# A new order of issue for the first 700 operations of an S4 and GEGLU block

## The chip, the cores and the metric

The kernel runs on one core of one Trainium2 chip. The metric is the time of one execution in device microseconds; the time of a kernel is the median of its runs.

## The reference

The input is a sequence of L = 2048 tokens with D = 448 channels. A conditioning vector gives six rows `sa, ca, ga, sb, cb, gb` (a SiLU and one matrix product). The block has two halves:

```
mod = (silu(c) @ w_mod)                          # 6 rows of 448
h = layernorm(x) * (1 + ca) + sa
# S4: a convolution of length 2048 for each channel
P = exp(dt * A * l)                              # 448 x 256 complex states x 2048 steps
K = einsum("dn,dnl,dn->dl", C, P, dt * B).real
y = irfft(rfft(pad(h)) * rfft(pad(K)))[:L] + h * Dskip
x = x + ga * y
h = layernorm(x) * (1 + cb) + sb
x = x + gb * ((gelu(h @ w_gate) * (h @ w_up)) @ w_down)
```

Everything is float32 from outside. The costly parts are the generation of K (complex exponentials for 448 channels and 256 states), the Fourier transforms as matrix products, and the GEGLU with its 1792 hidden features.

## The kernel before

**What is computed when.** The channels are taken eight at a time, in 56 steps `s` (`NSUB`); seven steps make a group `sc`, and two groups share one `prep(t)`, t = 0 to 3. The parts that the first 700 operations come from:

- `prep(t)` turns the complex parameters of 112 channels into the logarithms and phases that the exponentials need. It is a ladder of short steps that hop between VectorE (DVE) and ScalarE (ACT): `p.A1`, `p.A2`, `p.B1`, `p.C2`, `p.D1`, `p.B3`, `p.G1`, `p.E1`, `p.E3` on DVE; `p.S1`, `p.S2` (a logarithm), `p.S3` (an exponential), `p.S4` (an arctangent), `p.A3`, `p.C1`, `p.B2`, `p.E2` on ACT. Its two results are split in three bfloat16 pieces each (`p.c0` to `p.f0`, `p.c1` to `p.f1`; the casts `c` and `e` may run on either engine) and stored to HBM by `p.put0` and `p.put1` beside a constant `pad`. The text calls these steps `A1`, `S1` and so on.
- `load_lt(sc)` (`lt0`, `lt1`) reads them back, rearranged, as matmul operands. `lt0` waits for `p.put0` and for `pad`.
- For each step, TensorE (PE) multiplies them with constants into exponents (`x.mm`, `y.mm`) and angles (`ang`, `anc`); ACT takes exponentials (`x.exp`, `y.exp`) and sines (`sin`, `cos` and, for the first 20 steps, `sin2`, `cos2`); DVE multiplies (`tx`, `tyc`); PE contracts over the states (`kgen`). `kev`, `kd`, `ka` and `kout` turn a pair of steps into spectra of the first kind.
- `mod_row(i)` loads a part of `w_mod` (`m.ld`), multiplies (`m.mm`, or `m.mq0`, `m.cp0` and a sum `m.sm0`) and evacuates (`m.ev`). The products `gs` of two such rows scale the layer norm.
- The tokens: `x.ld`, statistics `bn` on DVE, a square root `rstd` on ACT, `rcp`, `norm` and a scaled constant `as`, the matmuls `ua`, the evacuations `ua.ev`, stores `ua.st`; then the second stage of the transform: `ub.u`, `ub.fc`, `ub`, `ub.ev` or `ub.eg`, `ub.st`.

Behind them follow the spectral products group by group (`f.*`, `t.*`), and then the GEGLU, which fills the rest of the span.

**What sets the order.** There are 2006 operations, and each is issued at a place written out in the table `PLACE`: the n-th number of a name is the place of its n-th call. `Plan.run` sorts by it and issues each operation with all its instructions, so each engine, and the queue of DMA issues on SyncE (SP), gets its own in this order and waits at the head for what is missing.

```
at = PLACE[n][i]
self.at, e = int(at.rstrip("adps")), at[-1]
self.on = {"a": "ACT", "d": "DVE", "p": "POOL", "s": "SP"}.get(e) or next(iter(eng))
```

So a letter behind a number chooses the engine of an operation that may run on two. Buffers are taken and freed in the same order. ACT holds one set of function tables at a time: exponentials, sines and arctangents, the logarithm and the square root are in four sets here, and where the next function is not in the set, a load of a table (`ACT_TABLE_LOAD`) stands ahead of it. Copies, squares and absolute values need none.

Of the kernel before, what the change touches and what calls it, by code (L numbers as in the profile page):

```python
# [40 lines left out]
    "anc": "127 138 148 162 173 210 218 246 266 319 327 332 359 351 433 450 484 460 499 483",  # L41
    "ang": "110 113 140 158 168 164 207 221 247 312 323 331 347 350 423 444 459 448 498 476 508 584 615 595 665 680 663 703 "
        "747 763 768 791 795 815 782 883 889 928 904 914 938 946 1012 1028 1019 1040 1045 1054 1116 1133 1142 1148 1163 "
        "1169 1175 1196",
    "as": "65d 58d 80d 105d 115d 120d 156a 146d 254d 252d 282d 296d 321a 317a 341a 353a",
    "bn": "20 45 24 40 15 17 48 16 215 216 238 245 157 220 194 190",
    "c.ai": "133",
    "c.ak": "231",
    "c.au": "47",
    "c.c": "8",  # L50
    "c.ea": "57",
    "c.ih": "516",
    "c.ld": "4",
    "c.rd": "51",
    "c.t1": "363",
# [21 lines left out]
    "cos": "522 592 638 616 672 699 700 712 762 776 789 814 808 819 796 894 910 942 907 922 945 952 1016 1037 1022 1048 1060 "  # L77
        "1068 1127 1137 1153 1160 1172 1183 1207 1229",
    "cos2": "128 141 152 163 178 211 219 253 272 320 328 343 360 354 440 451 490 467 505 488",
# [3 lines left out]
    "d0": "172",  # L83
# [21 lines left out]
    "dsk": "174",  # L105
# [10 lines left out]
    "ev.ub": "397",  # L116
# [9 lines left out]
    "gs": "66 86",  # L126
# [17 lines left out]
    "ka": "240 279 316 355 381 406 495 525 606 603 710 718 737 832 812 880 917 930 974 1001 1064 1080 1135 1166 1194 1206 "  # L144
        "1242 1246",
    "kd": "200 232 291 346 379 398 469 519 575 579 677 706 736 831 806 879 898 926 970 984 1032 1076 1129 1152 1193 1200 "
        "1240 1245",
    "kev": "199d 230d 290a 345a 378d 393a 462a 518d 548a 577a 654a 705a 735d 818d 805d 853d 897d 924d 969d 983d 1030d 1075d "
        "1113d 1140a 1162a 1191a 1239d 1236a",
    "kgen": "145 181 206 228 243 273 297 322 344 372 376 390 412 419 466 491 517 547 563 576 634 635 679 702 721 722 755 772 "  # L150
        "783 799 822 838 859 896 900 923 937 957 955 982 1025 1026 1049 1058 1086 1105 1128 1139 1158 1161 1181 1190 1199 "
        "1218 1223 1235",
    "kout": "241a 280a 318d 371a 394d 461a 496a 527a 620a 636d 716a 728d 749a 848a 813d 887d 925a 933a 979a 1003a 1069d 1102a "
        "1141a 1167a 1195a 1222a 1244a 1247a",
    "lt0": "64 144 325 368 560 801 861 985",
    "lt1": "92 195 326 369 723 802 968 986",
    "m.cp": "581a 600d 786a",
    "m.cp0": "50d",
    "m.ev": "44 60 63 589 619 804",
    "m.ld": "29 31 30 420 578 760",  # L160
    "m.mm": "43 59",
    "m.mq": "555 599 773",
    "m.mq0": "46",
    "m.sm": "588 618 803",
    "m.sm0": "62",
    "mag": "511a 591a 617a 598d 670d 689a 668a 708a 752d 764a 770a 792a 797d 816a 784a 892a 890d 929a 905a 915a 943a 947a "
        "1013a 1029a 1020d 1041a 1052a 1055a 1117d 1134a 1143a 1149a 1164a 1170a 1185a 1209a",
    "norm": "67 70 99 109 97 121 72 104 237 249 281 287 171 278 227 285",
    "p.A1": "1 88 311 509",
    "p.A2": "7 89 349 531",  # L170
    "p.A3": "25 169 456 481",
    "p.B1": "13 103 365 554",
    "p.B2": "22 155 438 607",
    "p.B3": "23 177 439 613",
    "p.C1": "6 98 416 478",
    "p.C2": "14 106 435 553",
    "p.D1": "32 134 426 571",
    "p.E1": "39 167 437 673",
    "p.E2": "41 185 489 674",
    "p.E3": "42 187 506 686",  # L180
    "p.G1": "38 125 436 623",
    "p.S1": "11 102 358 532",
    "p.S2": "18 116 373 569",
    "p.S3": "21 132 413 570",
    "p.S4": "37 166 434 626",
    "p.al": "2 33 91 474",
    "p.c0": "26a 204d 470a 627a",
    "p.c1": "49a 191d 530d 696d",
    "p.d0": "27 250 493 647",
    "p.d1": "52 258 611 738",  # L190
    "p.e0": "28a 289d 494a 701d",
    "p.e1": "53d 259a 612d 833d",
    "p.f0": "34 298 502 717",
# [1640 lines left out]
```

## Time and profile before

| | |
|---|---|
| median of 3 runs | 777.25 us (776.79 to 779.4) |
| the profiled execution | 776.06 us, of it a span of 774.3 us from the first to the last instruction |
| granted clock of TensorE, mean | 0.995 |
| busy: PE, DVE, ACT | 724.2, 591.3, 459.7 us |
| DMA | 139.87 MB, 181 GB/s over the span |

A row of a group has line, engine, operation, tiles and shapes, the count, then busy us and the mean ns of one, and behind the bar the idle time ahead of them and what ended it. A row of the view in order of time has start and length in us, and in brackets an idle time of the engine ahead of it. A row of the waits has the engine and line that waited, what it waited for, us in total, times and the longest. A row of DMA issues has its size and the us from issue to landing. `q` behind an engine's name is its sequencer; PEld are PE's loads of stationary operands.

### The profile page before, as it was taken

What the parts mean: (1) busy time and instruction counts of PE and PEld (TensorE: products, weight loads), DVE (VectorE), ACT (ScalarE), POOL (GpSimd) and SP (SyncE); (2) the same over time, 40 slices, a digit from 0 to 9 for tenths busy, and PEclk for the clock granted to TensorE, in tenths of its full rate; (3) what the DMA queues carried; (4) which work ended last, traced back from release to release, by engine and by line L of the source; (5) the groups of instructions that cost most, each with busy time, mean ns of one, the idle gap of its engine ahead of it and who ended that gap; (6) DMA issues with size and microseconds to landing.
All of it is one profiled execution on the core that took longest, in us unless ns stands there. A gap on an engine that the chain in (4) does not pass through costs nothing.

```text
span 774.3 us, 19010 instructions
## 1 busy us (share of the span) xinstructions
PE 724.2 (94%) x8166; PEld 442.5 (57%) x8166; DVE 591.3 (76%) x891; ACT 459.7 (59%) x613; POOL 8.5 (1%) x23
## 2 busy tenths in 40 slices
PE   2877889998899999989999999999999999999997
PEld 1333554443677777677874445444694446944487
DVE  6999999999999999979958932578774577144743
ACT  5899999999999999952646620244312433022330
POOL 0000000000000000003000000000000000000000
PEclk9999999999999999999999999999999999999999
DMA  9764777997888687897787791455247224013201
GB/s 265 193 187 160 214 184 222 276 272 236 247 230 252 180 233 239 275 310 208 235 269 257 221 235 79 146 166 211 98 82 211 96 96 136 14 50 99 77 2 60
DMA packets 103950, 139.87 MB, mean 181 GB/s; under 512 B 34388, under 2 KB 85492, under 8 KB 103866
## 3 DMA queue, kind: packets, MB, share of 16 engines
q1 hardware_dynamic: 100436, 132.53, 58.2%
q10 hardware_dynamic: 2950, 5.38, 2.0%
q8 instruction: 64, 1.05, 0.6%
q0 software_dynamic: 480, 0.75, 0.3%
q14 instruction: 20, 0.16, 0.1%
HBM read 100.39 MB, written 36.01 MB: 176 GB/s over the span
## 4 chain that ended last, share of the span: by engine, by line
PE 73%; ACT 12%; DVE 8%; DMA 4%; issue 2%; SPq 1%; DVEq 0%; ACTq 0%
PE pq L1530 32%; PE pq L1630 9%; PE pd L1599 4%; PE pg L676 4%; PE pf L1104 4%; PE kg L749 3%; ACT my L663 3%; DVE ty L726 2%; PE pq L1524 2%; PE pf L985 2%; PE pf L1093 2%; PE kg L772 2%; PE pf L1206 2%; ACT fg L689 2%; DMA us<-uo 2%
## 5 line engine op out<-in xcount | busy, mean ns | idle before, releaser
L1530 PE MATMUL pq<-ht,wr 128*128 128x512 f16 (+1 forms) x1200 | 248.3, 365 | 0.1
L1530 PEld LDWEIGHTS <-wr 128*128 128x128 f16 x1200 | 114.6, 98 | 128.5 <-issue 11.3
L726 DVE TENSOR_TENSOR ty<-my,fg 128x2048 f32<-128x2048 f32 x56 | 127.3, 2284 | 0.4 <-ACT fg L693 0.3
L1537 ACT ACTIVATE ge<-pq 128x512 f32<-128x512 f32 (+1 forms) x60 | 34.0, 566 | 106.9 <-PE pq L1524 71.3
L1544 DVE TENSOR_TENSOR fq<-ge,pq 128x512 f32<-128x512 f32 (+1 forms) x60 | 39.0, 650 | 72.6 <-PE pq L1530 45.0
L1556 ACT ACTIVATE hh<-fq 128x1024 f16<-128x1024 f32 (+1 forms) x49 | 46.7, 962 | 65.6 <-DVE fq L1544 47.0
L1630 PE MATMUL pq<-d,hh 128*128 128x224 f16 x476 | 68.9, 259 | 0.0
L722 DVE TENSOR_TENSOR tx<-mx,fg 128x1024 f32<-128x1024 f32 x56 | 67.6, 1218 | 0.2 <-ACT fg L700 0.2
L749 PE MATMUL kg<-ty,tx 128*32 128x64 f32 x3584 | 61.6, 222 | 4.4 <-DVE tx L722 1.7
L749 PEld LDWEIGHTS kg<-ty,tx 128*32 128x32 f32 x3584 | 53.2, 111 | 21.3 <-issue 5.9
L1559 DVE TENSOR_TENSOR hlo<-fq,hh 128x1024 f16<-128x1024 f32 (+1 forms) x49 | 53.7, 1106 | 12.9 <-ACT hh L1556 12.7
L1630 PE MATMUL pq<-d,hlo 128*128 128x224 f16 x238 | 61.6, 259 | 0.0
L689 ACT ACTIVATE fg<-pg 128x1024 f32<-128x1024 f32 x56 | 57.6, 1040 | 0.5 <-PE pg L676 0.3
L663 ACT ACTIVATE my<-pg 128x1024 f32<-128x1024 f32 x56 | 56.2, 1032 | 0.4
L1630 PEld LDWEIGHTS <-hh 128*128 128x128 f16 x560 | 54.1, 98 | 0.9 <-issue 0.2
L693 ACT ACTIVATE fg<-fg,small 128x1024 f32<-128x1024 f32 x36 | 42.2, 1180 | 0.0
L1104 PE MATMUL pf<-q,fc 128*128 128x160 f32 x264 | 41.5, 307 | 0.0
L1104 PEld LDWEIGHTS pf<-q,fc 128*128 128x128 f32 x264 | 36.5, 190 | 5.3 <-issue 2.2
L676 PEld LDWEIGHTS <-lt 64*128 64x128 bf16 x304 | 17.7, 95 | 35.0 <-issue 22.7
L676 PE MATMUL pg<-ea,lt 64*128 64x512 bf16 x152 | 31.3, 390 | 6.5 <-ACT fg L689 3.0
L1747 ACT ACTIVATE d<-fq 128x896 f16<-128x896 f32 x14 | 13.2, 946 | 39.7 <-PE pd L1599 27.3
L985 PE MATMUL pf<-ui,fu 128*128 128x448 f32 x66 | 31.2, 576 | 1.2 <-DVE uo L993 0.5
(210 smaller groups left out, 1119.2 us busy)
## 6 DMA issues: line engine op xcount, KB each, us to landing
wr<-w_d SPq DMA_DIRECT2D x21, 896.0 KB, 4.6
fc<-in_k_fc SPq DMA_DIRECT2D x20, 576.0 KB, 4.2
u_d<-so SPq DMA_DIRECT2D x32, 224.0 KB, 3.0
ui<-u_d SPq DMA_DIRECT2D x10, 672.0 KB, 6.0
fq<-in_wd SPq DMA_DIRECT2D x14, 448.0 KB, 4.1
w<-in_wgu SPq DMA_DIRECT2D x11, 512.0 KB, 4.6
us<-uo SPq DMA_DIRECT2D x22, 240.0 KB, 4.5
q<-us SPq DMA_DIRECT2D x22, 240.0 KB, 4.5
```

The costliest lines, as they stand in the source:

```text
L663: A.activation(yb.tile.rearrange("p h (n k) -> p n h k", n=2), pb.tile.rearrange("p (n h k) -> p n h k", n=2, h=2), AF.Exp)
L676: T.matmul(pa[:, nh * 512:nh * 512 + 512], w, x, start=(k == 0), stop=(k == 2))
L689: A.activation(fb.tile[:, 0].rearrange("p x (n k) -> p n x k", n=2), pb.tile.rearrange("p (n x k) -> p n x k", n=2, x=2), AF.Sin, scale=TW ...
L722: V.tensor_mul(tx.tile, xb.tile[:, xm, None, :].to_broadcast([128, 2, 512]), fb.tile[:, :, 0])
L726: V.tensor_mul(ty.tile, yb.tile[:, :, None, :].to_broadcast([128, 2, 2, 512]), fb.tile[:, None, :, 1].to_broadcast([128, 2, 2, 512]))
L749: T.matmul(kg[32 * g:32 * g + 32, 2 * (s % 2) + q, :64], tx[:, r, nh, 4 * q + g], ty[:, 0:4:3, nh, 4 * q + g] if r else ty[:, 1:3, nh, 4 * ...
L985: T.matmul(pb.tile, fu.tile[:, i], ui.tile[:, EORD[e0 + i] % 32 - s0], start=True, stop=True)
L1104: T.matmul(pz.tile[:, e % 32 - sl0], fc.tile[:, i, 1 + t], pp.tile[:, t, i], start=(t == 0 and e != 32), stop=(t == 1 and e != 0))
L1530: T.matmul(pb.tile[k][:, ts], wr.tile[:, 4 * lo + t, k, c0:c0 + 128], ht[:, m, ts], start=f % 2 == 0 and i == 0, stop=f % 2 == 1 and i == 9)
L1556: A.activation(hg.tile[0][:, cb, c], fq.tile[:, c], AF.Copy)
L1559: V.tensor_sub(hg.tile[1][:, cb, c], fq.tile[:, c], hg.tile[0][:, cb, c])
L1630: T.matmul(bank(k)[:, m], x[:, p, q[0], ts], w[:, p, q[1]], start=new and m == 0 and p == 0 and z == 0, skip_group_check=True, stop=i in ( ...
```

## The change

The table `PLACE` gets new numbers for the operations at places 0 to 699; it is the same set of 700, and the operations from 700 on keep their places. Of the 700, 39 keep theirs too. Half are moved by 6 places or less; the largest moves are `pad` of the second `prep` (100 to 297), `c.t1` (363 to 193), `d0` (172 to 6) and `x1.ld` (286 to 191). 29 operations change engine between ACT and DVE; after it, 201 of the 700 are on ACT (202 before) and 213 on DVE (212 before). No instruction is added or taken away but table loads, which follow from ACT's order. The diff, cut to the names above (the places of matmuls, sines, products and of the second transform stage are left out):

```diff
...
-"as": "65d 58d 80d 105d 115d 120d 156a 146d 254d 252d 282d 296d 321a 317a 341a 353a",
-"bn": "20 45 24 40 15 17 48 16 215 216 238 245 157 220 194 190",
...
-"c.ak": "231",
-"c.au": "47",
-"c.c": "8",
-"c.ea": "57",
...
+"as": "65d 72d 109d 88d 133d 131d 165d 152a 250d 254d 285d 260a 318d 317d 338d 360a",
+"bn": "18 25 19 29 43 45 44 46 218 219 229 222 157 227 197 159",
...
+"c.ak": "195",
+"c.au": "64",
+"c.c": "3",
+"c.ea": "60",
...
-"c.rd": "51",
-"c.t1": "363",
+"c.rd": "57",
+"c.t1": "193",
...
-"d0": "172",
+"d0": "6",
...
-"dsk": "174",
+"dsk": "161",
...
-"gs": "66 86",
+"gs": "62 96",
...
-"kev": "199d 230d 290a 345a 378d 393a 462a 518d 548a 577a 654a 705a 735d 818d 805d 853d 897d 924d 969d 983d 1030d 1075d "
+"kev": "188a 277d 270d 331a 388d 399d 448a 485a 564a 591a 646a 705a 735d 818d 805d 853d 897d 924d 969d 983d 1030d 1075d "
...
-"kout": "241a 280a 318d 371a 394d 461a 496a 527a 620a 636d 716a 728d 749a 848a 813d 887d 925a 933a 979a 1003a 1069d 1102a "
+"kout": "220a 304d 298d 374d 476a 402a 521a 546a 617d 641a 716a 728d 749a 848a 813d 887d 925a 933a 979a 1003a 1069d 1102a "
...
-"lt0": "64 144 325 368 560 801 861 985",
-"lt1": "92 195 326 369 723 802 968 986",
-"m.cp": "581a 600d 786a",
-"m.cp0": "50d",
-"m.ev": "44 60 63 589 619 804",
-"m.ld": "29 31 30 420 578 760",
-"m.mm": "43 59",
-"m.mq": "555 599 773",
-"m.mq0": "46",
-"m.sm": "588 618 803",
-"m.sm0": "62",
...
+"lt0": "69 123 342 369 589 801 861 985",
+"lt1": "87 211 368 406 723 802 968 986",
+"m.cp": "558a 607d 786a",
+"m.cp0": "58d",
+"m.ev": "34 61 68 580 612 804",
+"m.ld": "32 35 36 417 593 760",
+"m.mm": "33 54",
+"m.mq": "548 602 773",
+"m.mq0": "55",
+"m.sm": "579 611 803",
+"m.sm0": "67",
...
-"norm": "67 70 99 109 97 121 72 104 237 249 281 287 171 278 227 285",
-"p.A1": "1 88 311 509",
-"p.A2": "7 89 349 531",
-"p.A3": "25 169 456 481",
-"p.B1": "13 103 365 554",
-"p.B2": "22 155 438 607",
-"p.B3": "23 177 439 613",
-"p.C1": "6 98 416 478",
-"p.C2": "14 106 435 553",
-"p.D1": "32 134 426 571",
-"p.E1": "39 167 437 673",
-"p.E2": "41 185 489 674",
-"p.E3": "42 187 506 686",
-"p.G1": "38 125 436 623",
-"p.S1": "11 102 358 532",
-"p.S2": "18 116 373 569",
-"p.S3": "21 132 413 570",
-"p.S4": "37 166 434 626",
...
-"p.c0": "26a 204d 470a 627a",
-"p.c1": "49a 191d 530d 696d",
-"p.d0": "27 250 493 647",
-"p.d1": "52 258 611 738",
-"p.e0": "28a 289d 494a 701d",
-"p.e1": "53d 259a 612d 833d",
-"p.f0": "34 298 502 717",
-"p.f1": "61 284 637 845",
-"p.ld": "0 3 83 84 201 260 314 475",
-"p.put0": "36 300 536 744",
-"p.put1": "71 288 685 873",
-"pad": "35 100 261 750",
-"rcp": "55 251",
-"rstd": "54 248",
-"sel": "56",
-"sil2": "12",
-"silu": "9",
...
+"norm": "66 81 63 92 132 77 117 101 249 246 245 230 241 240 253 291",
+"p.A1": "2 89 316 526",
+"p.A2": "12 94 321 527",
+"p.A3": "11 115 431 480",
+"p.B1": "16 110 351 534",
+"p.B2": "23 141 428 574",
+"p.B3": "28 190 429 578",
+"p.C1": "13 99 416 490",
+"p.C2": "14 100 427 619",
+"p.D1": "26 151 420 586",
+"p.E1": "40 174 445 656",
+"p.E2": "41 200 460 657",
+"p.E3": "47 201 470 690",
+"p.G1": "37 111 430 644",
+"p.S1": "15 107 350 533",
+"p.S2": "21 112 365 535",
+"p.S3": "22 136 389 571",
+"p.S4": "27 173 440 621",
...
+"p.c0": "30a 259a 432d 630d",
+"p.c1": "48d 214d 475a 697a",
+"p.d0": "31 268 439 658",
+"p.d1": "51 244 561 738",
+"p.e0": "38d 272d 441d 701d",
+"p.e1": "52a 265a 622d 833d",
+"p.f0": "39 286 515 717",
+"p.f1": "59 301 637 845",
+"p.ld": "1 10 71 80 226 293 329 477",
+"p.put0": "42 287 516 744",
+"p.put1": "76 339 691 873",
+"pad": "53 297 294 750",
+"rcp": "50 248",
+"rstd": "49 247",
+"sel": "0",
+"sil2": "9",
+"silu": "7",
...
-"ua": "74 81 112 118 135 151 175 192 255 263 283 303 329 336 364 375",
-"ua.ev": "75d 76d 82d 85d 114d 117d 119d 122d 149a 143a 160a 154a 182d 180d 193a 197a 257a 256a 264a 269a 295d 299a 305a "
-        "309a 330a 333a 339d 337a 370d 366d 380d 377a",
...
-"ub.ev": "447a 457a 458a 485a 510a 514a 542a 562d 582a 604d 625a 633d 653a 676d 684a 694a",
...
+"ua": "78 90 114 120 134 149 179 189 252 261 288 306 327 335 361 373",
+"ua.ev": "85d 86d 95d 91d 118d 119d 121d 122d 146a 148a 166a 153a 185d 181d 198a 208a 256a 258a 264a 266a 290a 303a 307a "
+        "310a 328a 330a 348a 337a 366d 362d 379d 375a",
...
+"ub.ev": "451a 459a 461a 492a 510a 525a 530d 559a 583a 610d 625a 633d 655a 670a 674a 696a",
...
-"x.exp": "90 111 77 96 189 203 205 244 374 411 402 543 552 586 641 656 719 730 753 727 858 854 840 874 863 978 963 1007 "
+"x.exp": "104 106 73 98 192 202 183 239 378 405 394 555 563 577 640 650 719 730 753 727 858 854 840 874 863 978 963 1007 "
...
-"x.ld": "19 10 214 139",
-"x.mm": "87 107 73 95 188 202 198 242 367 410 400 540 551 585 640 655 707 729 751 726 852 851 839 870 862 975 959 1006 "
+"x.ld": "17 24 217 156",
+"x.mm": "102 103 70 97 186 187 182 235 377 404 393 553 562 576 639 649 707 729 751 726 852 851 839 870 862 975 959 1006 "
...
-"x1.ld": "286 1463 1661 1782",
...
+"x1.ld": "191 1463 1661 1782",
...
```

56 rows, old and new, of the table PLACE are left out of this document.

## The prediction

> **What bounds the kernel now.** I read the page first (busy shares and the chain that ended last), then stretches cut where the change ends, then the waits of VectorE (DVE) and ScalarE (ACT) in those stretches, and last the first 30 us instruction by instruction.
>
> From the page: the span, the busy times of the engines, and the chain by engine.
>
> ```profile
> span 774.3 us, 19010 instructions
> ...
> PE 724.2 (94%) x8166; PEld 442.5 (57%) x8166; DVE 591.3 (76%) x891; ACT 459.7 (59%) x613; POOL 8.5 (1%) x23
> ...
> PE 73%; ACT 12%; DVE 8%; DMA 4%; issue 2%; SPq 1%; DVEq 0%; ACTq 0%
> ```
>
> TensorE (PE) carries the chain, but that is a sum over stages. Operations 0 to 699 are issued in the first quarter of the span: the last of them on DVE is the `tyc` multiplication of the first row below, which ends at 190.43 us. So the windows view, in the other rows, is cut there. Its columns are the stretch, its length, the busy time of PE, PE's weight loads, DVE, ACT and POOL with their instruction counts, then granted clock, DMA share and GB/s.
>
> ```profile
> 188.15 2.28 DVE L726 TENSOR_TENSOR ty<-my,fg 128x2048 f32<-128x2048 f32 x1
> ...
> 0.00:25.20 25.20, 9.72 (x26) 4.21 (x26) 18.17 (x47) 14.41 (x24) 0.88 (x10) 1.00 0.88 257
> 25.20:190.50 165.30, 143.31 (x2273) 72.02 (x2273) 160.72 (x215) 162.88 (x217) 0.00 (x0) 0.98 0.76 215
> 27.20:187.00 159.80, 138.59 (x2176) 69.00 (x2171) 155.25 (x208) 157.55 (x211) 0.00 (x0) 0.98 0.76 216
> 190.50:341.00 150.50, 143.30 (x2912) 107.84 (x2915) 147.56 (x152) 141.91 (x163) 0.00 (x0) 1.00 0.83 244
> ```
>
> The reader is to see three things. Before 25.2 us DVE and ACT have holes (7.0 and 10.8 us idle): a start-up of short dependent steps. From there to 190.5 us DVE is idle for 165.30 - 160.72 = 4.58 us, and ACT from its first exponential at 27.2 to the last operation of the first 700 at 187 for 159.80 - 157.55 = 2.25 us. PE has 22 us to spare there. From 190.5 to 341, where the order stays, DVE has the least idle time (2.94 us, against 7.2 on PE and 8.6 on ACT). So the first 700 operations are worth what DVE, and next to it ACT, need to get through them, and a shift there is handed on almost whole to a stage in which no engine can absorb it.
>
> Where do those 4.58 and 2.25 us sit? The waits view for each engine: DVE's longest and its shortest of ten rows, and ACT's longest of three.
>
> ```profile
> DVE so L483 <- PE pf L922: 1.3, 4, 0.4
> ...
> DVE tx L722 <- ACT fg L700: 0.2, 1, 0.2
> ACT so L481 <- PE pf L922: 0.5, 3, 0.2
> ```
>
> No wait is long; the worst place costs 1.3 us in four pieces. An order can win little here, and lose more.
>
> **The change part by part.** Work. The set of the first 700 is the same in both orders, so PE and the DMAs do the same work. Two things differ. Twenty-nine operations that may run on either engine change sides, and the sequence of functions on ACT needs 25 table loads instead of 26 (counted along ACT's order: the logarithm `S2` of the fourth `prep` stood amid exponentials, at 569, and now stands at 535, where ACT goes from sines to exponentials anyway). The durations by shape:
>
> ```profile
> L912 DVE TENSOR_SCALAR as<-au,rs 128x128 f32<-128x128 f32 x11 | 3.0, 281 | 0.2
> L910 ACT ACTIVATE as<-au,rs 128x128 f32<-128x128 f32 x5 | 2.0, 400 | 0.0
> L483 DVE COPY so<-pf 128x448 f32<-128x448 f32 x15 | 9.0, 620 | 1.3 <-PE pf L922 1.3
> L481 ACT ACTIVATE so<-pf 128x448 f32<-128x448 f32 x17 | 8.9, 550 | 0.6 <-PE pf L922 0.5
> L483 DVE CAST lh<-q 112x512 bf16<-112x512 f32 x9 | 3.8, 418 | 0.1
> L481 ACT ACTIVATE lh<-q 112x512 bf16<-112x512 f32 x7 | 4.5, 647 | 0.9 <-DVE q L537 0.8 <-DVE q L579 0.2
> L483 DVE COPY ako<-kg 128x512 f32<-128x512 f32 x7 | 4.8, 683 | 0.0
> L481 ACT ACTIVATE ako<-kg 128x512 f32<-128x512 f32 x21 | 12.8, 611 | 2.8 <-PE kg L772 2.0 <-issue 0.8
> ```
>
> Net moves: two `as` and one `kout` (ako) and one `p.c`/`p.e` cast (lh) from ACT to DVE; two `ua.ev` (so) and one `ub.ev` of the same shape from DVE to ACT; `kev` trades evenly. DVE: 2 x 0.281 + 0.683 + 0.418 - 3 x 0.620 = -0.20 us. ACT: -(2 x 0.400 + 0.611 + 0.647) + 3 x 0.550 = -0.41, and one table load less at 1.28 us (row below): -1.69 us.
>
> Start-up. These rows carry it (instructions in order of time, and issues to landing):
>
> ```profile
> 6.73 0.42 DVE L549 TENSOR_TENSOR q<-q 112x256 f32<-112x256 f32 x1
> 7.38 0.19 ACT L793 ACTIVATE sig<-c_sb 112x4 f32<-112x4 f32 x1
> 7.47 0.61 ACT L552 ACTIVATE q<-q 112x512 f32<-112x512 f32 x1
> 8.02 0.16 DVE L798 TENSOR_TENSOR c_sb<-c_sb,sig 112x4 f32<-112x4 f32 x1
> 12.17 0.42 ACT L571 ACTIVATE q<-q 112x256 f32<-112x256 f32 x1
> 14.95 0.42 DVE L574 SCALAR_TENSOR_TENSOR q<-q 112x256 f32<-112x256 f32 x1
> 17.54 0.68 DVE L539 TENSOR_TENSOR lh<-q,lh 112x512 bf16<-112x512 f32 x1
> 20.33 0.62 DVE L878 BATCH_NORM_STATS2 st<-xt 128x6 f32<-128x448 f32 x1
> 21.09 0.59 DVE L878 BATCH_NORM_STATS2 st<-xt 128x6 f32<-128x448 f32 x1
> 24.38 0.92 PE L823 MATMUL pf<-zo,small 128*128 128x448 f32 x2
> 25.16 0.63 DVE L860 TENSOR_TENSOR gs<-gs,rows 128x448 f32<-128x448 f32 x1 [0.46 <-ACT gs L834]
> 25.34 0.54 ACT L831 ACTIVATE gs<-pf 128x448 f32<-128x448 f32 x1 [0.21 <-PE pf L823]
> 25.90 1.28 ACT L663 ACT_TABLE_LOAD   x1
> 27.19 1.02 ACT L663 ACTIVATE my<-pg 128x1024 f32<-128x1024 f32 x1
> 5.88 0.65 SPq L515 DMA_DIRECT2D lh_d<-in_k_one  x1
> 18.25 0.33 SPq L596 DMA_DIRECT2D lh_d<-lh  x1
> 22.05 1.34 SPq L621 DMA_DIRECT2D lt<-lh_d  x2
> lh_d<-lh SPq DMA_DIRECT2D x2, 336.0 KB, 3.7
> q<-in_abc SPq DMA_DIRECT2D x2, 224.0 KB, 5.7
> DMA to landing us min/median/max: 3.2/3.4/4.6
> 25.23 0.09 PEld L658 LDWEIGHTS <-lt 64*128 64x128 bf16 x1 [0.65 <-DMA lt<-lh_d]
> ```
>
> (a) Before, `A2` ended on DVE at 6.73 + 0.42 = 7.15 and `sil2` behind it at 8.18. The new order swaps them. `sil2` waits for `silu` (7.38 now; it moves ahead of `C1`, to about 6.5), so the pair is through at about 8.1, and ACT's `S1`, which reads `A2` and now also stands behind `A3`, starts at about 8.1 instead of 7.47: +0.65. `B1`, `S2`, `S3` follow step by step, so `S3` ends at 12.59 + 0.65 = 13.25.
>
> (b) `D1` used to start at 14.95, 2.4 us after `S3` was ready, since two `bn`, `B3` and `d0` were queued ahead. Now three `bn` fill the time and `D1` starts when `S3` ends, at about 13.3, after some 1.1 us of idle DVE. It gives 1.65 us back, but `B3`, one `bn` (0.76 from start to start), `d0`, `G1` and a cast stand between it and `f0`: `f0` ends at about 18.9 instead of 17.54 + 0.68 = 18.22. +0.7.
>
> (c) Behind `f0` stand four `bn` instead of three, but `G1` and two `as` less: equal work within 0.1 us, so 18.9 + 6.5 = 25.4. The cast `e1`, which `f1` reads, moves to ACT (0.65 us instead of 0.42) with only `m.cp0` to cover it; I add 0.4. `gs` starts at about 25.8 instead of 25.16: +0.6 on DVE.
>
> (d) `m.cp0` goes behind the `bn` on DVE and ends at about 25.2, one `f1` ahead of `gs`; PE's sum behind it (0.92 us, L823) ends at about 26.1, and the last start-up evacuation on ACT starts there instead of at 25.34. With the same table load behind it, the first exponential starts at 27.9 instead of 27.19: +0.7 on ACT.
>
> (e) The queue on SP: `pad` (5.88) is moved behind `p.put0`, which itself waits for `f0`. The put then goes out at 18.95 and `pad` at 19.3 to 19.95; landing like the put, in 3.7 us, it lets `lt0` go at about 23.7 instead of 22.05, and its two halves are in by 27.2 (25.2 and 25.6 before). With 0.5 us of matmuls that is 27.7, hidden behind ACT's 27.9 by 0.2 us. The loads `x1.ld`, `c.t1` and `c.ak` also move on SP, to an emptier stretch; I cost them at nothing, since the ACT and DVE work of (c) to (d) covers their issue times and nothing near them reads them.
>
> The sum to the boundary. DVE: +0.6 from the start, and behind `gs` the work is -0.20 less what fell ahead of it (-0.16): -0.04. So +0.6. ACT: +0.7, and of its -1.69 one cast of 0.65 fell ahead of the first exponential, which leaves -1.04: -0.3. The waits in between are unknown in the new order. Their ends: all of DVE's 4.58 us gone (-4.6; ACT could follow by 2.25 only), or as much again (+4.6). I take them as unchanged, since the producer and consumer distances that I compared shrink in some places (`x.ld` now stands directly ahead of its first `bn`) and grow in others. DVE, with the least idle time behind the boundary, decides: +0.6 us. The profiled execution took 776.06 us (774.3 us of span and 1.8 around it), 1.2 us under the median of the runs shown: 776.7 for it, and 777.25 + 0.6 = 777.9 us for the median. A difference under 0.3%, 2.3 us, is about what a measurement of this kernel can't tell from none (the three runs lie 2.6 us apart).
>
> **The rivals.** First, ACT and not DVE sets the boundary. For it: ACT idles less in the middle (2.25 against 4.58 us). Against it: behind the boundary ACT has 8.6 us to spare. Its sum is -0.3: 776.9 us.
>
> The Trainium skill ("ScalarE: Activation LUTs", section "What ACT_TABLE_LOAD costs") says that every switch to another set costs a drain of about 1380 ns beside the load of 1283 ns, about 2.66 us in all. By that ACT would save 1.4 us more and the time by this rival would be 775.5 us. The trace does not agree: the load at 25.90 takes 1.28 us, and the exponential behind it starts at 27.19, so nothing is left for a drain.
>
> Second, the waits shrink. For it: they are many and short, the kind a shifted neighbour removes. Against it: the longest single one shown is 0.4 us, and the start costs 0.6 first. Half of DVE's gone gives 777.25 + 0.6 - 2.3 = 775.6; for faster by over 0.3% at least 2.9 of DVE's 4.58 us must go and all that ACT has: 774.5, at the very best 773.3.
>
> Third, slower, by one mechanism: `pad` behind `p.put0`. The cover in (e) is 0.2 us. If `pad` lands as the 224 KB load `q<-in_abc` does, 5.7 us after issue, then `lt0` goes at 25.6, and the first exponential waits 1.9 us more, with every multiplication on DVE behind it: 777.25 + 0.6 + 1.9 = 779.8 us. It decides from the point where `lt0` is issued later than 23.9 us.
>
> Fourth, the same side without one place: the tight distances turn into waits and DVE's idle time doubles, 782 us.
>
> **How the numbers follow.** DVE decides with the waits as they are: 0.35 (777.9). ACT decides: 0.15 (776.9). Waits shrink by about half: 0.10 (775.6). All these are within 0.3%: 0.60. Waits nearly gone: 0.15, faster. `pad` late: 0.12, and waits doubled: 0.13, slower together 0.25. A tenth of the chance is left out on each side: 774.6 to 781.5 us.
>
> **What would show it right or wrong.** In the changed kernel's trace: the first exponential at about 27.9 us and `gs` at about 25.8; one ACT table load less up to the boundary; `f0` ending near 18.9; `lt0` issued near 23.7, and PE's first matmul on `lt` no later than 27.3. DVE's idle time from `gs` to the boundary near 4.6 us and ACT's near 2.3. A first exponential before 27 us would say that (a) and (b) are wrong; one at 29 or later, that `pad` is late. An idle time of DVE under 2 us or over 8 us would make the sum wrong, whatever the start does.

## The result, and the profile after

The new order makes the kernel slower: 783.07 us median (15 runs, 780.1 to 788.42) against 778.42 for the kernel before on the same chip (15 runs, 775.08 to 781.49), a ratio of 1.0059 with a 95% interval of 1.004 to 1.0079. That is 4.65 us, outside the predicted range and on the side that had a quarter of the chance. The profiled execution took 783.1 us, at the median of its runs; that of before (776.06 us) lies 2.4 us under the median that its longer series shows now. So the two traces lie 7.0 us apart where the medians lie 4.65 apart, and a difference between the two traces is not in full the order's.

The page of the new kernel: the span, the busy times and the chain that ended last, by engine.

```profile
span 781.3 us, 19016 instructions
...
PE 724.8 (93%) x8166; PEld 443.1 (57%) x8166; DVE 590.6 (76%) x892; ACT 458.3 (59%) x611; POOL 8.5 (1%) x23
...
PE 78%; ACT 7%; DVE 5%; DMA 3%; issue 2%; SPq 0%; ACTq 0%; DVEq 0%
```

The work is what the prediction counted: ACT's busy time falls by 1.4 us (1.69 forecast), DVE's by 0.7 (0.20 forecast). So the time that was lost went into waiting. The windows view (columns as in the prediction) says where.

```profile
25.20:190.50 165.30, 139.71 (x2182) 69.86 (x2182) 155.46 (x212) 156.73 (x210) 0.00 (x0) 0.96 0.74 211
190.50:341.00 150.50, 143.04 (x2905) 106.35 (x2904) 146.64 (x150) 146.29 (x170) 0.00 (x0) 1.00 0.81 236
```

From 25.2 to 190.5 us DVE is idle for 165.30 - 155.46 = 9.84 us, where it was 4.58; ACT for 8.57 where it was 2.42. Behind 190.5 DVE is idle for 3.86 us (2.94 before). The idle time of the middle has doubled, and that is 5.3 of DVE's lost microseconds. The waits of DVE in that stretch, in full:

```profile
DVE so L483 <- PE pf L922: 2.3, 3, 0.8
DVE uo L993 <- PE pf L985: 1.7, 2, 1.3
DVE tx L722 <- ACT fg L700: 1.1, 1, 1.1
DVE q L537 <- ACT lh L481: 1.0, 1, 1.0
DVE ke L767 <- ACT ke L481: 0.9, 1, 0.9
DVE rs L890 <- ACT rs L887: 0.7, 1, 0.7
DVE q L579 <- ACT q L578: 0.5, 1, 0.5
DVE as L912 <- DMA au<-in_k_au: 0.2, 1, 0.2
```

Before, the longest place cost 1.3 us in four pieces of 0.4 at most. Now single waits of 0.7 to 1.3 us stand there, and they name every partner: late products of PE and late results of ACT.

The start-up, in the view in order of time, answers the prediction's steps (a) to (e):

```profile
18.55 0.69 DVE L539 TENSOR_TENSOR lh<-q,lh 112x512 bf16<-112x512 f32 x1
25.77 0.62 DVE L860 TENSOR_TENSOR gs<-gs,rows 128x448 f32<-128x448 f32 x1
15.18 8.38 PE L816 MATMUL pf<-fg,c_sb 112*128 112x448 f32 x16 [15.18 <-DMA fg<-in_w_mod]
23.49 0.96 PE L812 MATMUL pf<-fg,c_sb 112*32 112x448 f32 x8
25.28 0.99 PE L823 MATMUL pf<-zo,small 128*128 128x448 f32 x2 [0.84 <-DVE zo L483]
27.64 0.28 PE L639 MATMUL pg<-rd,lt 64*128 64x256 bf16 x1 [1.37 <-DMA lt<-lh_d]
26.31 0.54 ACT L831 ACTIVATE gs<-pf 128x448 f32<-128x448 f32 x1 [0.74 <-PE pf L823]
28.52 1.02 ACT L645 ACTIVATE mx<-pg 128x1024 f32<-128x1024 f32 x1 [0.36 <-PE pg L639]
23.49 1.34 SPq L621 DMA_DIRECT2D lt<-lh_d  x2
```

`f0` ends at 19.24 (18.9 forecast), `gs` starts at 25.77 (25.8), `lt0` goes out at 23.49 (23.7). PE's first matmul on `lt` starts at 27.64 instead of 27.2, so PE waits 1.37 us for the load, and the first exponential starts at 28.52 instead of 27.9: the 0.2 us of cover in (e) were not there. The load itself was not issued late; PE's first matmul on it starts 4.15 us behind the issue, where the forecast had 3.5 (and the trace of before 3.2). In this trace the start is 1.33 us late on ACT, twice the 0.7 of the forecast. It still explains less than a third of the 4.65 us.

### The profile page after: what moved, and what is told of

Its sections match the earlier page's. It is cut to its first block, busy times and chain, and to the rows that moved or that the text cites. A ratio compares the mean times of both kernels' runs of the same rounds, so it can differ in the third digit from the quotient of the medians.

```text
span 781.3 us, 19016 instructions
## 1 busy us (share of the span) xinstructions
PE 724.8 (93%) x8166; PEld 443.1 (57%) x8166; DVE 590.6 (76%) x892; ACT 458.3 (59%) x611; POOL 8.5 (1%) x23
## 4 chain that ended last, share of the span: by engine, by line
PE 78%; ACT 7%; DVE 5%; DMA 3%; issue 2%; SPq 0%; ACTq 0%; DVEq 0%
PE pq L1530 31%; PE pq L1630 9%; PE kg L749 6%; PE pg L676 5%; PE pf L1104 4%; PE pd L1599 4%; PE kg L772 3%; PE pf L985 3%; PE pf L1093 2%; PE pq L1524 2%; PE pf L1206 2%; PE pd L1630 2%; DVE ty L726 1%; DMA us<-uo 1%; ACT my L663 1%
## 5 line engine op out<-in xcount | busy, mean ns | idle before, releaser
L749 PE MATMUL kg<-ty,tx 128*32 128x64 f32 x3584 | 62.2, 222 | 7.3 <-issue 2.7
L749 PEld LDWEIGHTS kg<-ty,tx 128*32 128x32 f32 x3584 | 53.5, 111 | 24.9 <-issue 14.8
```

The lines of the kernel that those rows point to most:

```text
L749: T.matmul(kg[32 * g:32 * g + 32, 2 * (s % 2) + q, :64], tx[:, r, nh, 4 * q + g], ty[:, 0:4:3, nh, 4 * q + g] if r else ty[:, 1:3, nh, 4 * ...
```

## The experiments

### Old and new order by parts

The theories at first: (A) TensorE's granted clock is halved more often in the new order, and its late products make the waits; (B) results are used too soon after they are made, everywhere; (C) all of the loss comes from the start. The first 700 places were cut into three parts: start (0 to 70), middle (70 to 420), end (420 to 700). The kernels take the operations of a part in the old or the new order, with the engine that this order gives them:

```diff
 first all operations with a place below the cut, by the first order's places;
 then all others, by the second order's places
-# kernel after: new | new | new        kernel before: old | old | old
+# new_to_70:  new | old | old          old_to_70:  old | new | new
+# new_to_420: new | new | old          old_to_420: old | old | new
+# middle_new: old | new | old          middle_old: new | old | new
+# new_to_250: new to place 250, old from there
```

**new_to_70.** 

> The first 70 operations in the new order, all others in the old one's order. Theory A (the new order's early matmuls leave TensorE idle, its granted clock is halved in more stretches between 20 and 80 us, and the late matmuls make the waits): the halved stretches lie behind this part, so about +0.5 us, no more than the start-up costs. Theory B (the new order puts producers too close ahead of their consumers all along the first 190 us, whatever the clock is): the start-up's +0.6 us as well. Rival C (the whole loss comes from the start, handed on): +4 us or more.

**new_to_250.** 

> The first 250 operations in the new order (to about 75 us), all others in the old one's order. Theory A (halved clock between 20 and 80 us): nearly the whole loss, +3.5 to +4.6 us, and a mean granted clock of 0.991 to 0.993 as with the whole change. Theory B (short distances everywhere): the share of DVE's new idle time that lies before 75 us, 2 of 5 us: +1.5 to +2.5 us.

**new_to_420.** 

> The first 420 operations in the new order (to about 120 us), all others in the old one's order. Theory A: the whole loss, +4 to +4.6 us. Theory B: DVE's new idle time before 120 us is 3 to 3.5 of 5 us: about +3 us.

**old_to_420.** 

> The first 420 operations in the old order, the others of the first 700 in the new one's order. Theory A (halved clock between 20 and 80 us): no loss, 0 +- 1 us, and a mean granted clock of 0.995. Theory B: the waits that the new order has behind 120 us (DVE 1.1 us more for PE's second stage at 125.8, 0.9 for `ke` at 160.4, 1.0 for a store at 191.2) are here alone: +1.5 to +2.5 us.

**old_to_70.** 

> The first 70 operations in the old order, 70 to 700 in the new one. The traces show the new start 0.6 us later on VectorE and 0.7 us on ScalarE at the end of the start-up walk. Theory B: about 0.6 us comes back, 782.5 us. Rival C (the start costs what new_to_70 showed, 2.3 us): about 780.8 us. Theory A: whichever of the two, the half-speed stretches decide, and differ from run to run.

**middle_new.** 

> Old order of the first 70 operations, new order of 70 to 420, old order from there. Theory G (the loss of 4.6 us is 2.3 us in the start and some 2.5 us at 150 to 196 us, the part between costs nothing): 777.7 to 778.4 us, VectorE's idle time at 150 to 196 us about 0.3 to 0.6 us. If the new order costs by short hand-overs everywhere: 780 us or more. If it is the change from one order to the other that costs: two such places, 781 us.

**middle_old.** 

> New order of the first 70 operations, old order of 70 to 420, new order of 420 to 700: the eighth combination. If the parts add up (start 1.9 us, middle 0.3, end 2.2): 4.1 us above the kernel before, 782.4 us where that takes 778.3, with VectorE idle for some 3 to 4 us at 150 to 196 us. If the start's delay is taken up by waits of the end that were there anyway: 2.5 us above it, 780.8.

Measured, with the idle time of DVE at 150 to 196 us from the windows view of each trace ("before" is the median of the old order in the same series; the ratio comes with its interval from the single runs and is not the quotient of the two medians):

| start, middle, end | kernel | median us | before | ratio (95%) | DVE idle 150 to 196 us |
|---|---|---|---|---|---|
| new, old, old | new_to_70 | 780.49 | 778.16 | 1.0033 (1.0018 to 1.0048) | 0.32 |
| old, new, old | middle_new | 779.77 | 778.24 | 1.0014 (0.9997 to 1.0031) | 0.27 |
| new, new, old | new_to_420 | 779.49 | 778.16 | 1.0027 (1.0003 to 1.005) | 0.37 |
| old, old, new | old_to_420 | 782.43 | 778.16 | 1.0051 (1.0032 to 1.007) | 4.02 |
| old, new, new | old_to_70 | 780.8 | 778.71 | 1.0018 (1.0001 to 1.0035) | 3.06 |
| new, old, new | middle_old | 785.3 | 778.88 | 1.0094 (1.0072 to 1.0116) | 3.90 |
| new, new, new | the new order | 783.07 | 778.42 | 1.0059 (1.004 to 1.0079) | 3.04 |
| old, old, old | the old order | | | 1 | 0.57 |

Each part can be read from four pairs that differ in it alone. The new start costs 0.33, 0.13, 0.43 and 0.41%, in the mean 2.5 us. The new end costs 0.51, 0.04, 0.61 and 0.32%, in the mean 2.9 us. The new middle costs 0.14, -0.06, -0.33 and -0.35%, in the mean -1.2 us: it gives back some of what a new end beside it costs. The sum is 4.2 us of the 4.65. A single pair is good to about 2 us, a mean of four to about 1. The start and the end nearly add up (0.33 and 0.51%, and 0.94 in middle_old, which has both); the middle does not add: beside an old end it costs 0.14 and -0.06%, beside a new one it gives 0.33 and 0.35% back. A least-squares fit to the single runs of all eight says much the same (start 2.3, middle 0.0, end 2.6 us, each within 0.7). So the start and the end carry the loss, and the middle carries none. Theory C falls as the whole and stands for half; A and B fall as far as they put the loss in the middle.

new_to_250 suggests that a seam between two orders can make waits of its own: 783.72 us, 1.0072 (1.0045 to 1.0098), although new_to_420, with more of the new order, is better. Its longest waits stand behind the seam: 2.8 us on ACT at 83.3 us (`so`) and 4.1 us on DVE at 92.7 us (`ke`). The kernels of the table have seams too, at places 70 and 420, and what those cost is not shown.

The end part shows in the windows view as a fixed feature of a kernel, not as scatter. The stretch from 150 to 196 us, first in the old order's trace, then in the new one's, new_to_420's and old_to_420's:

```profile
150.00:196.00 46.00, 41.17 (x706) 20.58 (x704) 45.43 (x58) 44.91 (x58) 0.00 (x0) 1.00 0.90 254
```

```profile
150.00:196.00 46.00, 42.04 (x710) 21.23 (x711) 42.96 (x52) 43.23 (x59) 0.00 (x0) 1.00 0.91 256
```

```profile
150.00:196.00 46.00, 42.45 (x642) 19.90 (x637) 45.63 (x59) 45.74 (x61) 0.00 (x0) 1.00 0.89 260
```

```profile
150.00:196.00 46.00, 41.12 (x709) 20.93 (x708) 41.98 (x50) 42.83 (x57) 0.00 (x0) 1.00 0.87 252
```

The third number behind the length is DVE's busy time: 45.4 and 45.6 of 46 us with the old end, 43.0 and 42.0 with the new one. Over all twenty traces, DVE is idle there for 0.27 to 0.57 us in the seven with the old end and for 1.38 to 5.55 us in the thirteen with the new one. All four ran with TensorE at the full granted clock there.

### Taking away single waits

A fourth theory came up in the traces: (D) TensorE's instructions arrive late behind 120 us.

**repair_both.** Each operation that its engine waited for in the new order's trace was moved behind neighbours that were ready. The larger moves:

```diff
 VectorE
-ua.ev 6, ua.ev 7, as 5, norm 4, as 4      ub.eg 0, p.C2 2, p.B3 2, p.G1 2, p.c0 2
+as 5, norm 4, as 4, ua.ev 6, ua.ev 7      p.C2 2, p.B3 2, p.G1 2, p.c0 2, ub.eg 0
-p.d0 1, tx 7     ua.ev 30, tx 11     kd 8, ub.eg 8, tyc 20
+tx 7, p.d0 1     tx 11, ua.ev 30     tyc 20, ub.eg 8, kd 8
 ScalarE
-ua.ev 16, ua.ev 17, p.c0 1, as 11, ua.ev 18, p.e1 1     y.exp 21, p.B2 2
+p.c0 1, as 11, p.e1 1, ua.ev 16, ua.ev 17, ua.ev 18     p.B2 2, y.exp 21
-y.exp 23, p.B2 3     cos 0, p.S1 3      p.S2 1, sin2 1, p.A3 1
+p.B2 3, y.exp 23     p.S1 3, cos 0      p.A3 1, p.S2 1, sin2 1
```

> The new order, with about twenty operations of VectorE and ScalarE between 30 and 165 us moved by one to five places: each operation that its engine waited for in the profile of the new order goes behind neighbours on the same engine that were ready, or the neighbours go ahead of it. TensorE's and SP's queues keep their order. Theory B (short hand-overs between the two full engines): the waits named hold some 6 us of VectorE's 9.84 us of idle time between 25.2 and 190.5 us and some 5 us of ScalarE's 7.81; they go, VectorE's idle time falls to about 5, and the kernel to about 779.5 us (3.5 us below the new order). Theory A (halved TensorE clock): the half-speed stretches stay, so the time stays within 1 us of 783. Theory D (late instruction fetches on TensorE behind 120 us): within 1 us of 783.

Measured: 784.14 us, 1.006 (1.004 to 1.0079). Nothing came back. The middle of its trace and its longest waits of DVE there:

```profile
25.20:190.50 165.30, 136.96 (x2180) 68.48 (x2172) 153.91 (x211) 155.19 (x208) 0.00 (x0) 0.97 0.71 205
```

```profile
DVE ke L483 <- PE kg L749: 3.1, 2, 2.4
DVE tx L722 <- ACT fg L700: 1.9, 1, 1.9
DVE uo L993 <- PE pf L985: 1.1, 2, 0.6
```

DVE is idle for 11.39 us there, more than the 9.84 it was to lose some 6 of. Several of the named waits are gone (`q` on `lh`, `ke` on `ke`, `q` on `q`), and others of the same size stand in their place.

**repair_vector**, only the moves on VectorE. 

> Only the moves of VectorE's operations of repair_both (eight operations). If VectorE's waits alone set the time of this stretch, all of the 3.5 us comes back (about 779.5 us). If the two engines hold each other, a half or less: about 781.5 us, because ScalarE's waits stay and return as waits of VectorE. Theories A and D: within 1 us of 783.

Measured: 782.09 us, 1.0046 (1.0026 to 1.0067).

**repair_scalar**, only the moves that take away ScalarE's waits. 

> Only the moves that take away ScalarE's waits (with three operations of VectorE put ahead that feed them). If ScalarE's waits set the time: about 779.5 us. If the two engines hold each other: about 781.5 us. Theories A and D: within 1 us of 783.

Measured: 782.83 us, 1.0054 (1.0032 to 1.0075). Neither is told apart from the new order's 1.0059. In these three kernels a wait that was taken away came back elsewhere, and theory B in the form "repair the waits" falls.

### TensorE's clock

**new_fill.** In the new order the trace shows PE sparse at 70 to 74 us and then halved for 6.8 us; the windows view, with the granted clock behind POOL's count:

```profile
70.00:74.00 4.00, 2.02 (x70) 1.32 (x70) 3.90 (x10) 3.97 (x6) 0.00 (x0) 1.00 0.63 210
74.10:80.90 6.80, 6.27 (x84) 3.22 (x81) 6.12 (x11) 5.87 (x7) 0.00 (x0) 0.50 0.01 2
```

The Trainium skill ("TensorE: Matmul & The Clock Gate", Part 1 on the clock gate) has a monitor that looks at windows of 3413 ns that run freely and passes half of the clock after one idle window. The stretches at half clock ahead of the span's end in these traces are multiples of 3.41 us, which agrees; but the 3.41 us ahead of this one were not empty: PE was busy for 44% of them. So the sparse stretch was filled:

```diff
-def ymm(s=s, pb=pb):
+def ymm(s=s, pb=pb, n=3 if len(MY) in (6, 7) else 1):
-    for nh in range(2):
+    for nh in list(range(2)) * n:
         T.matmul(pb.tile[...], lhs(s, 0, nh), row(ea, nh, 512, 1024), start=True, stop=True)
```

> The new order; the matmuls of the seventh and eighth y part (y.mm 6 and 7) are issued three times over the same PSUM buffer, 1.1 us more work for TensorE in the sparse stretch at 71 to 74 us, nothing else changed. Theory F (the new order of places 70 to 250 leaves TensorE sparse there, so that its clock is halved at 74 to 81 us, in seven of seven traces that hold this part, and its late products make waits): the halved stretch is gone, the way from the second rstd to the ninth ty product falls from 16.9 to 19.4 us to about 15.7 to 16.5, the mean halved time of a run from 12 to about 7 us, and the time at 0.39 us for each to about 781.2 us. Without it, or if the halved stretch stays: 783 us or up to 1 us more, for the added matmuls.

Measured: 783.9 us, 1.0081 (1.0053 to 1.0109). The same two stretches in its trace:

```profile
70.00:74.00 4.00, 2.50 (x78) 1.55 (x75) 3.86 (x10) 3.97 (x5) 0.00 (x0) 1.00 0.79 279
74.10:80.90 6.80, 4.67 (x90) 2.15 (x87) 6.00 (x12) 6.74 (x9) 0.00 (x0) 1.00 0.01 2
```

In the traced execution the clock stayed at full there, and the time is not lower. Over all its runs the time at half clock (from span and mean granted clock of each) is 11.2 us, against 12.2 for the new order: the edit hardly changed the clock, so this kernel does not test theory A.

**new_group_fill**, with the edit of new_group_back below. 

> Both edits of new_group_back and new_fill together. If E and F both hold and add up: about 780.3 us. If only one of them: 781.2 to 782.2. If neither: 783.

Measured: 782.59 us, 1.0063 (1.0041 to 1.0085).

**old_fill**, the same edit in the old order for y.mm 2 to 8. 

> The old order; the matmuls of seven y parts (y.mm 2 to 8, at 27 to 72 us) are issued three times, 4 us more work for TensorE, nothing else changed. Theory F, if halved stretches cost in the old order too (8.7 to 9.3 us of them in a mean run): they fall to about 4 us, and the time by 1 to 1.5 us to about 777 us, which beats both kernels. If the added matmuls delay the products that the two other engines wait for: 779.5 to 781 us.

Measured: 781.02 us, 1.003 (1.0011 to 1.0048): slower, although the runs spend 4.2 us at half clock instead of 9.2. The clock part of the expectation came true and the time went the other way, so the edit costs more than the clock gave. Whether the matmuls themselves cost it is open: the trace also has five of the stops of PE that the part on the end describes, 4.5 us in all, where the old order's trace has one of 1.5. Within the fit of the eight combinations a microsecond at half clock goes with 0.23 us of time; the new order has some 3 us more of it than the old one, which makes 0.7 us of the 4.65. So theory A is at most a small part.

### The start

**new_group_back.** In the new order the two groups of L816 run together and L812 behind them, so that the copy between L812 and the sum L823 is no longer covered (PE's 0.84 us in the fence of the start-up above). The old arrangement was put back:

```diff
 SP       -m.ld 0, m.ld 1, m.ld 2               +m.ld 0, m.ld 2, m.ld 1
 PE       -m.mm 0, m.mm 1, m.mq0, m.sm0         +m.mm 0, m.mq0, m.mm 1, m.sm0
 VectorE  -rcp 0, p.d1 0, m.cp0, p.f1 0         +m.cp0, rcp 0, p.d1 0, p.f1 0
```

> The new order with one part of its start put back: the four-part matmul group of line 812, its weights and its copy (m.mq, m.ld, m.cp) stand again between the two groups of line 816, so that the copy is hidden behind the second of them. Theory E (the start costs 2.3 us, as new_to_70 and old_to_70 showed, through TensorE's late groups): the sum over the copy (line 823), which ended at 26.3 to 28.0 us in the traces with the new start and at 25.3 to 26.1 with the old one, ends 0.8 to 1.2 us earlier; the first exponentials follow, and the time is about 782.2 us. If this group is all of the start's cost: 780.8 us. If the start's cost is elsewhere (order of VectorE and ScalarE): 783 us, with the sum earlier and the third exponential where it was.

Measured: 781.26 us, 1.0045 (1.0023 to 1.0067). PE in its trace:

```profile
20.14 0.96 PE L812 MATMUL pf<-fg,c_sb 112*32 112x448 f32 x8
21.03 3.27 PE L816 MATMUL pf<-fg,c_sb 112*128 112x448 f32 x8
24.14 0.92 PE L823 MATMUL pf<-zo,small 128*128 128x448 f32 x2
27.80 0.28 PE L639 MATMUL pg<-rd,lt 64*128 64x256 bf16 x1 [2.75 <-DMA lt<-lh_d]
```

The sum ends 1.2 us earlier, as expected, and nothing follows from it: PE then waits 2.75 us for `lt`, and the first exponential starts at 28.96 us. Behind the one late item stood the other, the load that waits for `pad`; it was issued at 22.69 us.

**start_mended.** Both were put back:

```diff
 as new_group_back, and on SP
-p.put0 0, pad 0, c.rd, c.ea
+pad 0, p.put0 0, c.rd, c.ea
```

> The new order; in the start, the group of line 812 with its weights and copy stands between the two groups of line 816 again, and pad stands ahead of p.put0 on SP's queue again; VectorE and ScalarE keep the new order but for that copy. Theory G with these two as the cause: the lt load is issued at about 21.9 us, the first matmuls on it start as soon as the sum has ended (25.2 to 26.2 us), the first exponential at 27.2 to 28.2 us, and the time is 780.8 us, as old_to_70. If the order of VectorE and ScalarE is the cause: 782 to 783 us.

Measured: 781.11 us, 1.0037 (1.0021 to 1.0054). PE in its trace:

```profile
25.13 0.92 PE L823 MATMUL pf<-zo,small 128*128 128x448 f32 x2
25.98 0.39 PE L639 MATMUL pg<-rd,lt 64*128 64x256 bf16 x4
```

No wait is left between the sum and the first matmul on `lt`, and the first exponential starts at 27.94 us.

**start_mended_to_420**, the same with the old end. 

> The new order up to 420 with the start mended as in start_mended (group of line 812 between the two of line 816, pad ahead of p.put0), the old order from 420. If these two operations are the whole cost of the start: 0.3 to 0.6 us above the kernel before, 778.8 us. If the order of VectorE and ScalarE in the start costs too: 780 us or more.

Measured: 780.58 us, 1.0037 (1.0018 to 1.0055), against 1.0027 for new_to_420. So in one pair the mended start gives 0.22% and in the other it takes 0.10%, neither beyond its interval. What the traces show is the first exponential: 27.19, 27.67, 28.03, 28.30 and 28.50 us in five traces with the old start, 28.22 to 30.82 (mean 29.33) in ten with the new one, and 27.94, 28.91 and 27.00 in the three with the start mended. The mean of the five is 27.94, so the new start is 1.4 us late there, and the two late items are part of it; where the rest of the start's 2.5 us comes from is not shown.

### The end

**end_mended.** Three moves where DVE and ACT wait in the new order's trace at 157 to 164 us:

```diff
 PE       -kgen 19, y.mm 23      +y.mm 23, kgen 19
 ScalarE  -x.exp 12, kev 8       +kev 8, x.exp 12
 ScalarE  -cos 0, p.S1 3         +p.S1 3, cos 0
```

> The new order with three moves at 148 to 163 us: y.mm 23 ahead of kgen 19 on TensorE, kev 8 ahead of x.exp 12 and cos 0 behind the fourth S1 on ScalarE. Theory G with these as the cause: VectorE's idle time at 150 to 196 us falls from 3.0 to 5.6 us to about 1.3 us, and the time by 1.5 to 2 us to about 781.3 us. If other operations then wait in their place: 783 us.

Measured: 781.58 us, 1.0033 (1.0018 to 1.0048), from 1.0059: 2.0 us, though the two intervals overlap. The waits went, and came back 8 us later; DVE in its trace:

```profile
160.16 0.17 DVE L767 TENSOR_TENSOR ke<-kg,d 128x4 f32<-128x4 f32 x1
...
163.83 0.42 DVE L579 TENSOR_TENSOR q<-q 112x256 f32<-112x256 f32 x1
...
168.84 0.68 DVE L993 SCALAR_TENSOR_TENSOR uo<-gs,t1c,pf 128x448 f32<-128x448 f32 x1 [2.01 <-PE pf L985]
```

**both_mended.** 

> The edits of start_mended and end_mended together. If they add up: about 779 us, within 0.2% of the kernel before. If only one works: 781. If neither: 783.

Measured: 781.15 us, 1.0039 (1.0019 to 1.0059). The two mends do not add up in time, although DVE's idle time at 150 to 196 us falls to 1.78 us in its trace (the stop described next lasted 0.18 us there).

A part of what makes the end late is seen in PE's rows and not in the moved operations. The new order's trace, then old_to_420's, then end_mended's, in order of time:

```profile
160.12 0.99 PE L749 MATMUL kg<-ty,tx 128*32 128x64 f32 x56
161.75 0.32 PE L749 MATMUL kg<-ty,tx 128*32 128x64 f32 x8 [0.65 <-issue]
162.00 0.39 PE L658 MATMUL pg<-ea,lt 64*128 64x512 bf16 x2
```

```profile
159.19 1.08 PE L749 MATMUL kg<-ty,tx 128*32 128x64 f32 x58
162.11 0.31 PE L749 MATMUL kg<-ty,tx 128*32 128x64 f32 x6 [1.84 <-issue]
```

```profile
161.41 0.98 PE L749 MATMUL kg<-ty,tx 128*32 128x64 f32 x54
164.05 0.38 PE L749 MATMUL kg<-ty,tx 128*32 128x64 f32 x10 [1.65 <-issue]
```

PE stops in the midst of one operation (kgen 19, 64 matmuls with all their operands there), for 0.65 to 1.84 us, waiting for nothing that the profile shows. Nine of the thirteen traces with a new end have this stop of over 0.35 us at this operation (one more has it shortly before, at L812), and none of the seven with an old end has a stop of that kind between 125 and 200 us. In the new order's trace y.mm 23 stands behind the stop, and ACT (0.89 us for it) and then DVE (0.47 us) wait in turn.

The trace also has the packets of the instruction queue, one of 16,384 bytes ahead of each such stop. In the new order the last packet ahead of it runs from 158.98 to 160.09 us, and PE goes on at 161.75; in old_to_420 from 159.09 to 160.48, and on at 162.11; in end_mended from 161.15 to 162.53, and on at 164.05. That is 1.66, 1.63 and 1.52 us behind the end of the packet. Of 51 such stops of over 0.35 us between 28 and 345 us in all traces, every one ends 1.23 to 1.66 us behind the end of a packet. The DMA view of the new order's trace for 158.9 to 160.2 us has that packet:

```profile
q8 instruction: 1, 0.02, 5.4%
```

The place of the stops says the same. A trace of the new order has 64 of these packets and 16,422 instructions of PE (matmuls, weight loads and waits), one packet for about every 256. Counted from the first instruction, each of the 51 stops stands at the same place of every 256, at remainder 193 or 194; of PE's 608 waits of over 0.35 us that something released, none does. So PE had run out of instructions at the end of a block of 256, which is theory D of the expectations above, in the end part. The Trainium skill ("Runtime: NRT & Kernel Launch", section "Instruction fetch mechanics") says that an engine fetches its instructions in blocks of 16 KiB while it runs and that crossing a block's end is mostly hidden. The size agrees, and so does "mostly": 51 of the 814 block ends between 28 and 345 us show such a stop.

How the order brings it about is read from the traces. In the eleven traces with the new end and no added matmuls, the last packet ahead of this place starts 0.7 to 2.9 us after PE has entered the block, and it lasts 0.9 to 1.5 us; a stop ends 1.2 to 1.7 us behind that. PE is through the block in 3.3 to 3.9 us there; in the six traces with the old end and no added matmuls it takes 4.9 to 5.2 us for the block of the same number. No kernel moves the block's end alone. The nearest are new_fill and new_group_fill, whose added matmuls shift every later end by 16 instructions: both stop at L812 (2.27 us at 157.42 and 0.85 us at 153.44), and only the second stops again at L749.

The stop is not the whole of the end. Two of DVE's waits there in the new order's trace, in order of time, and its longest from the waits view:

```profile
160.36 0.17 DVE L767 TENSOR_TENSOR ke<-kg,d 128x4 f32<-128x4 f32 x1 [0.91 <-ACT ke L481]
...
163.89 0.43 DVE L579 TENSOR_TENSOR q<-q 112x256 f32<-112x256 f32 x1 [0.47 <-ACT q L578]
```

```profile
DVE uo L993 <- DMA us<-uo: 1.0, 1, 1.0
```

The wait for `ke` is over before the stop begins, and it is 0.91 us in all six traces that have the new end unmended and no added matmuls. The wait of `q` follows the stop: in the same six it is 0.47 to 1.75 us, each time 0.1 to 0.2 us shorter than the stop. The wait for a store comes at 191 us. So the stop accounts for 0.5 of DVE's 3.0 us here and for up to 1.75 of 4.0 in old_to_420; the rest is mainly the order on ACT and a late store. What each is worth in the median is not shown.

## Why the prediction was wrong

**What held.** The work (ACT 1.4 us less, DVE 0.7 less), steps (a) to (d) of the start to within 0.4 us on DVE, and the issue of `lt0` (23.49 us, 23.7 forecast). Also that DVE and ACT decide in this stretch: their idle time grew by 5.3 and 6.2 us, where the two traces lie 7.0 us apart.

**The step that failed** is "the waits in between ... I take them as unchanged". DVE's idle time from 25.2 to 190.5 us went from 4.58 to 9.84 us, just beyond the upper end that the prediction gave for it (as much again). The fourth rival, idle time doubled and 782 us, is what came, at a chance of 0.13. It had been called one "without one place". The runs give it one: at 150 to 196 us DVE's idle time goes from 0.57 to 3.04 us, and this end part costs 2.9 us of time. Ahead of it the doubling is in part the luck of one trace: the 4.58 us on which the sum was laid are the least of all twenty traces. At 25.2 to 45 us DVE is idle for 1.08 us before and 2.91 after, but for 3.06 in old_to_420, which has the old order there, and the 1.7 us more between 45 and 150 us (2.93 and 4.62) belong to a part whose new order costs nothing in the table. The rows for 25.2 to 45 us, before, after and old_to_420:

```profile
25.20:45.00 19.80, 14.83 (x96) 5.96 (x99) 18.72 (x35) 19.39 (x23) 0.00 (x0) 0.91 0.70 179
```

```profile
25.20:45.00 19.80, 13.97 (x68) 5.95 (x69) 16.89 (x35) 17.27 (x22) 0.00 (x0) 0.83 0.58 158
```

```profile
25.20:45.00 19.80, 16.11 (x69) 7.01 (x68) 16.74 (x34) 17.73 (x22) 0.00 (x0) 0.74 0.57 157
```

**The start was undersized.** +0.6 us was forecast and 2.5 us is the mean of four pairs. Two reasons are seen. Step (e) had `lt0` hidden by 0.2 us; its data came 0.4 us later than forecast and were exposed (0.36 us on ACT here; in new_group_back, with the sum out of the way, PE's 2.75 us). This is not the third rival as it was put: `lt0` went out at 23.49 us, ahead of that rival's limit of 23.9, and the load took 4.15 us instead of 3.5. (With the 0.2 us of cover, that rival's wait of 1.9 us should have been 1.7.) And the walk was laid on one trace of the old order whose start was the earliest of five: first exponential at 27.19 us, the others at 27.67 to 28.50, since the first eight matmuls of L816 took 4.97 us there and 5.79 in old_to_420, where the granted clock reached full at 20.6 us and not at 19.0. The rows of before and old_to_420:

```profile
15.48 4.97 PE L816 MATMUL pf<-fg,c_sb 112*128 112x448 f32 x8 [15.48 <-DVE q L574]
```

```profile
15.51 5.79 PE L816 MATMUL pf<-fg,c_sb 112*128 112x448 f32 x8 [15.51 <-DMA fg<-in_w_mod]
```

**The saved table load** was worth nothing that can be seen: placed where ACT goes from sines to exponentials, `S2` of the fourth `prep` stands directly behind the DVE step that it reads, and ACT waits 1.06 us for it, most of the 1.28 us saved:

```profile
151.38 1.28 ACT L570 ACT_TABLE_LOAD   x1 [1.06 <-DVE q L559]
```

The range (774.6 to 781.5) was too narrow above by its own terms: its two slower cases gave 779.8 and 782, each alone. A late load and doubled waits together were not in it, and something of both came.

## What to carry to other kernels

Where two engines are over 97% busy and feed each other, a reordering is not costed by its work. The idle time of the stretch is the term that matters; read it from several traces, give it the width of a doubling, and look first at the places where a queue has a boundary that the order does not show: a load that ends at the same moment as the work meant to cover it, and a block of instructions that ends in a run of many short ones.

A wait that a trace names is where a delay comes to light, and need not be what makes it. Moving the waiting operation mostly moved the wait; exchanging whole parts of the order told which parts cost, and the windows view of idle time, compared over several kernels, told the part from the scatter.

A chain of steps read from one trace of a start should be laid on the spread of several, since this one's first exponential moved by 1.3 us with nothing changed ahead of it.

## What the runs showed of the hardware

- PE ran dry of instructions at the end of a block of 256: 51 stops of 0.35 to 3.3 us (the longest in both_mended, at 334.0 us) at 814 block ends, 46 of them amid the many short matmuls of L749 and L772, each ending 1.2 to 1.7 us behind the end of a packet of 16,384 bytes on the instruction queue. The old order's trace has one too, 1.49 us at 328.3.
- The same order met TensorE's half clock at different times: the old order up to place 420 had it first at 32.6 to 36.0 us in one trace and at 34.3 to 44.5 in another.
- A table load took 1.28 us with the next function starting behind it at once: in start_mended it starts at 26.64 us and the exponential at 27.94.
